# Forward order of a decode step's attention: two V quarters between the products, pair sums and second sums moved ahead, q chunks in halves

## The chip, the cores and the metric

The kernel runs on one core of one Trainium2 chip. The metric is the device time of one execution in microseconds; lower is better. Three executions of the kernel before are known, with a median of 1634.19 us.

## What is computed

The program takes one token through an attention layer and a small MLP mixer, both modulated by a condition vector, and returns the output and the gradients by nine of its inputs. Most of the work is attention over a cache, forward and backward:

```python
Hq, Hkv, Sk, Dh = (32, 32, 8192, 192)         # x is (1, 1, 640)
h = layernorm(x) * (1 + ca) + sa              # ca, sa, ga, ... from silu(c) @ w_mod
q = (h @ wq).reshape(B, Sq, Hq, Dh).transpose(0, 2, 1, 3)
scores = einsum('bhqd,bhkd->bhqk', q, k) * Dh ** (-0.5)
p = softmax(scores)
o = einsum('bhqk,bhkd->bhqd', p, v)
x = x + ga * (o.transpose(0, 2, 1, 3).reshape(B, Sq, Hq * Dh) @ wo)
```

The gradients of K and V are as large as the caches. For the gradient of q the backward part needs, for each head, the matrix sum over positions of p * v (outer) k. The kernel calls it M and makes it in the forward part, so that K is read once; V is read again in the backward part.

## The kernel before

A head's cache of 8192 positions lies as 128 partitions x 64 positions x 192 channels. It is loaded in two halves of 32 positions per partition (1,536 KB each), and V is used in four quarters of 16 positions.

The forward part is one loop of 34 steps (line 393). Step `i` has three heads in hand: `x` is head `i`, whose scores are made; `y` is head `i - 1`, whose softmax and most of whose M are made; `z` is head `i - 2`, whose M is finished. For `x`, each half goes through `dot_mul` (L265, VectorE: K times q over all channels, into the only buffer `prod`), `dot_half` (L270, VectorE: halves the channels), `dot_tree` (L276, TensorE: six matmuls with the identity that add 16 channels at a time in PSUM), and `dot_sum` (L280, VectorE: the last 16 channels). For `y`, `reduce_max` and a matmul `mx` (L418) bring the maximum to all partitions, `negm` (L423) and an exponential on ScalarE (L301) follow; then each V quarter is scaled by the weights in `scale_v`: nine positions on VectorE (L313), seven on ScalarE (L320), into one of three buffers `vs`. `m_quarter` multiplies it on TensorE with K, in three groups of 16 matmuls (L327, L331 for the channels above 128, and L335 for the sums of V itself), and accumulates in PSUM over the four quarters. `m_out` (L338 to L342, ScalarE) and `m_add` (L347, VectorE) take the finished M out.

In odd steps two finished heads form a pair: `pair_sums` (L365 to L367, sixteen small fp32 matmuls), `pair_o` (L372 to L376, VectorE: the reciprocal and o), `pair_ao` (L383, TensorE, copied out by ScalarE at L457) and `e_rows` with `e_rows_out` (L351, L356, and a small write on GpSimd's queue, L357: the weights as rows, for the backward part). All of `po`, `ao_ps`, `er_ps` and `mod_ps` share one PSUM slot. In every fourth step `q_chunk` (L243, L245) makes the q of four heads, two at a time; its PSUM slot is that of `mx`. In steps 1, 5 and 9 `mod_blocks` (L218) makes a part of the modulation instead.

TensorE, VectorE and ScalarE run their instructions in the order in which the code states them: the loop stands in `manual_schedule`. The loads (SyncE's queue, SP in the profile) and GpSimd's queue are ordered by the framework's planner, which goes by its own estimate of when buffers come free. There are five K halves (`KB`), three V halves (`v_sb`), one buffer for a weights chunk (`w_st`) and two for `wo`. So the first K half of head `i + 1` can be loaded when M quarter 3 of head `i - 2` is done, its second one after M quarter 1 of head `i - 1`; V half 0 of head `i` after V quarter 3 of head `i - 2` is scaled, V half 1 of head `i` after V quarter 1 of head `i - 1` is scaled.

In a step, VectorE's order before is: sum of the last half, max, first product, negm, halving, V quarter 0, second product, M add, V quarter 1, second halving, V quarter 2, (pair_o), sum of the first half, V quarter 3. TensorE's is: mx, M quarter 3, first sums, M quarter 0, M quarter 1, (pair sums), second sums, M quarter 2, (AO, rows), (q or modulation).

The backward part (from line 599 on) streams V in and the gradients of V and K out. It isn't touched.

Of the kernel before, what the change touches and what calls it, by code (L numbers as in the profile page):

```python
# [8 lines left out]
FP32 = mybir.dt.float32  # L9
BF16 = mybir.dt.bfloat16  # L10
ALU = mybir.AluOpType
ACT = mybir.ActivationFunctionType
# [8 lines left out]
def kernel(  # L21
# [27 lines left out]
    P = 128  # L49
    D = A_x.shape[-1]  # L50
    _, HQ, S, DH = A_k_cache.shape
# [7 lines left out]
    ND = D // P  # L59
    NF = F // P  # L60
    NQ = QD // P
    NMB = NMOD // P
    NT = HQ // 2
    PW = 2 * DH
    CW = 2 * PW
    VW = DH + 4
    MW = DH + 1
    SCALE = DH ** -0.5
# [3 lines left out]
    V_, A_, T_ = nc.vector, nc.scalar, nc.tensor  # L72
# [7 lines left out]
    psB = ctx.enter_context(tc.tile_pool(name="psB", bufs=1, space=PS))  # L80
# [99 lines left out]
    def load_w(view3, lo, hi):  # L180
        w = wst.tile([P, ND, CW], BF16, name="w_st", tag="w", bufs=1)
        nc.sync.dma_start(out=w[:, :, 0 : hi - lo], in_=view3[:, :, lo:hi])
        return w
# [52 lines left out]

    qs_bc = const.tile([P, QD], BF16, name="qs_bc")

    def q_chunk(n, w):
        for b in range(2):  # L240
            ps = psB.tile([P, 512], FP32, name="q_ps", tag="b")
            for k in range(ND):
                T_.matmul(ps[:, 0:PW], lhsT=ha_bf[:, k : k + 1].to_broadcast([P, P]), rhs=w[:, k, b * PW : (b + 1) * PW], start=(k == 0), stop=(k == ND - 1))  # L243
            lo = n * CW + b * PW
            A_.activation(out=qs_bc[:, lo : lo + PW], in_=ps[:, 0:PW], func=ACT.Copy, scale=SCALE)  # L245

# [9 lines left out]
    def load_v(h, t):  # L258
        v = vp.tile([P, JH, DH], BF16, name="v_sb")
        nc.sync.dma_start(out=v, in_=V_hd[h][:, t * JH : (t + 1) * JH, :])  # L260
        return v
# [24 lines left out]
    with tc.tile_pool(name="kp", bufs=1) as kp, tc.tile_pool(name="vs", bufs=3) as vsp, tc.tile_pool(name="ft", bufs=2) as ft, \  # L286
# [20 lines left out]
        def scale_v(q, v, E4, Ef):  # L307
            vs = vsp.tile([P, JQ, VW], BF16, name="vs")
            j0 = q * JQ
            v0 = (q % 2) * JQ  # L310
            n = JQ - NVA
            A_.copy(out=vs[:, :, DH:VW], in_=E4[:, j0 : j0 + JQ, :])
            V_.tensor_tensor(  # L313
                out=vs[:, 0:n, 0:DH].rearrange("p j (a b) -> p j a b", b=4),
                in0=v[:, v0 : v0 + n, :].rearrange("p j (a b) -> p j a b", b=4),
                in1=E4[:, j0 : j0 + n, None, :].to_broadcast([P, n, DH // 4, 4]),
                op=ALU.mult,
            )
            for k in range(n, JQ):
                A_.activation(out=vs[:, k, 0:DH], in_=v[:, v0 + k, :], func=ACT.Copy, scale=Ef[:, j0 + k : j0 + k + 1])  # L320
            return vs

        def m_quarter(q, kb, vs, mp, op):
            j0 = (q % 2) * JQ
            z = q == 3
            for k in range(JQ):
                T_.matmul(mp[:, 0:MW], lhsT=kb[:, j0 + k, 0:P], rhs=vs[:, k, 0:MW], start=(q == 0 and k == 0), stop=(z and k == JQ - 1), skip_group_check=True)  # L327

            for k in range(JQ):
                p0 = 64 * (k % 2)  # L330
                T_.matmul(mp[p0 : p0 + 64, MO : MO + MW], lhsT=kb[:, j0 + k, P:DH], rhs=vs[:, k, 0:MW], start=False, stop=(z and k >= JQ - 2), skip_group_check=True)  # L331

            for k in range(JQ):
                p0 = 32 * (k % 4)
                T_.matmul(op[p0 : p0 + 32, 0:MW], lhsT=ones_bf, rhs=vs[:, k, 0:MW], start=(q == 0 and k < 4), stop=(z and k >= JQ - 4), skip_group_check=True)  # L335

        def m_out(h, mp, op, os_):
            A_.copy(out=M1[:, h, :], in_=mp[:, 0:MW])  # L338
            mt = ft.tile([P, MW], FP32, name="mt", bufs=1)
            A_.copy(out=mt[64:128, :], in_=mp[64:128, MO : MO + MW])  # L340
            os_[h] = ft.tile([P, MW], FP32, name="osb")
            A_.copy(out=os_[h], in_=op[:, 0:MW])  # L342
            return mt
# [42 lines left out]


        ORDER = {mybir.EngineType.PE, mybir.EngineType.DVE, mybir.EngineType.Activation}
        q_chunk(0, load_w(wq_v, 0, CW))
        mb = MB0  # L390
        X, os_, wo_l = {}, {}, {}
        with tc.manual_schedule(engines=ORDER):
            for i in range(HQ + 2):
                x = X[i] = {} if i < HQ else None
                y = X.get(i - 1) if 0 < i <= HQ else None
                z = X.pop(i - 2) if i > 1 else None
                wch = None
                if x is not None:
                    x["k"] = [load_k(i, 0), load_k(i, 1)]
                    x["v"] = [load_v(i, 0)]  # L400
                    x["S"] = ft.tile([P, J], FP32, name="S_h")
                    qh = qs_bc[:, i * DH : (i + 1) * DH]
                    if i % 2 == 0:
                        wo_l[i // 2] = load_wo(i // 2)
                if i % 4 == 3 and i + 1 < HQ:
                    wch = load_w(wq_v, ((i + 1) // 4) * CW, ((i + 1) // 4 + 1) * CW)
                if i % 4 == 1 and mb < NMB:
                    nb = min(CW // P, NMB - mb)
                    wch = load_w(wm_v, mb * P, (mb + nb) * P)
                if y is not None:  # L410
                    dot_sum(y["d1"], y["S"][:, JH:J])
                    m1 = tcol(1, "m1")
                    V_.reduce_max(out=m1, in_=y["S"], axis=AX.X)
                if x is not None:
                    pa = dot_mul(x["k"][0], qh)
                if y is not None:
                    mx = psB.tile([P, P], FP32, name="mx", tag="b")
                    T_.matmul(mx, lhsT=m1[:, 0:1].to_broadcast([P, P]), rhs=ident_f, start=True, stop=True)  # L418
                if z is not None:
                    m_quarter(3, z["k"][1], z["vs"], z["mp"], z["op"])  # L420
                if y is not None:
                    negm = tcol(1, "negm")
                    V_.reduce_max(out=negm, in_=mx, axis=AX.X, negate=True)  # L423
                    E4, Ef = softmax(i - 1, y["S"], negm)
                if x is not None:
                    dot_half(pa)
                    x["d0"] = dot_tree(pa, psR, DH // 2)
                if y is not None:
                    y["mp"] = psM.tile([P, 512], FP32, name="mp")
                    y["op"] = psO.tile([P, 256], FP32, name="op")  # L430
                    vs = scale_v(0, y["v"][0], E4, Ef)
                if z is not None:
                    mt = m_out(i - 2, z["mp"], z["op"], os_)
                if y is not None:
                    m_quarter(0, y["k"][0], vs, y["mp"], y["op"])
                if x is not None:
                    pb = dot_mul(x["k"][1], qh)
                if z is not None:
                    m_add(i - 2, z["mp"], mt)
                if y is not None:  # L440
                    vs = scale_v(1, y["v"][0], E4, Ef)
                    m_quarter(1, y["k"][0], vs, y["mp"], y["op"])
                if x is not None:
                    x["v"].append(load_v(i, 1))
                last = z is not None and i % 2 == 1
                t = (i - 3) // 2
                if last:
                    po = pair_sums((os_.pop(i - 3), os_.pop(i - 2)))
                if x is not None:
                    dot_half(pb)  # L450
                    x["d1"] = dot_tree(pb, psR, DH // 2)
                if y is not None:
                    vs = scale_v(2, y["v"][1], E4, Ef)
                    m_quarter(2, y["k"][1], vs, y["mp"], y["op"])
                if last:
                    o2 = pair_o(t, po)
                    A_.copy(out=AO[:, :, 2 * t : 2 * t + 2], in_=pair_ao(o2, wo_l.pop(t)))  # L457
                    e_rows_out(t, e_rows(t))
                if wch is not None:
                    if i % 4 == 3:  # L460
                        q_chunk((i + 1) // 4, wch)
                    else:
                        mod_blocks(mb, nb, wch)
                        mb += nb
                if x is not None:
                    dot_sum(x["d0"], x["S"][:, 0:JH])
                if y is not None:
                    y["vs"] = scale_v(3, y["v"][1], E4, Ef)
            while mb < NMB:
                nb = min(CW // P, NMB - mb)  # L470
                mod_blocks(mb, nb, load_w(wm_v, mb * P, (mb + nb) * P))
                mb += nb
# [353 lines left out]
```

## Time and profile before

| | |
|---|---|
| median of three executions | 1634.19 us (1628.32 to 1635.94) |
| the profiled execution | 1626.54 us |
| its span | 1624.7 us |
| busy: PE, DVE, ACT, POOL | 1251.1, 1110.5, 894.3, 108.0 us |
| share of the 16 DMA engines' time: loads, writes | 54.4%, 34.0% |
| read, written | 347.74 MB, 226.43 MB |
| product K times q (L265), 128 x 6144 | 3355 ns each, 64 times |
| V scaling on DVE (L313), one quarter | 1052 ns each, 128 times |

PE is TensorE's matmul side, PEld its weight loads, DVE VectorE, ACT ScalarE, POOL GpSimd, SP SyncE. A line number is that of the kernel before. A wait is idle time of an engine just ahead of an instruction, put down to what released it; idle time of an engine that isn't the bottleneck costs nothing. The clock is the share of full speed that TensorE was granted. Busy time of matmuls is modelled, since they overlap.

### The profile page before, as it was taken

The numbers are of one execution on the slowest core, as the hardware profiler recorded it, in microseconds if no ns is written. First come the engines' busy times: TensorE is split into PE (matmuls) and PEld (weight loads), VectorE is DVE, ScalarE is ACT, GpSimd is POOL, SyncE is SP. The second block draws the span as 40 slices with busy tenths as digits, with TensorE's granted clock in tenths as the row PEclk, the third lists the DMA queues.
The fourth block names the chain that finished last, engine by engine and source line by source line (L and its number), as shares of the span: only waits on it lengthen the run. The fifth ranks groups of instructions, "written<-read, shape, count | busy, mean of one in ns | idle before, by whom it ended". The sixth has DMA issues, their size and how long they took to land.

```text
span 1624.7 us, 28236 instructions
## 1 busy us (share of the span) xinstructions
PE 1251.1 (77%) x11811; PEld 665.3 (41%) x11811; DVE 1110.5 (68%) x1273; ACT 894.3 (55%) x1948; POOL 108.0 (7%) x193
## 2 busy tenths in 40 slices
PE   3888888888888888855784887878677878778774
PEld 1666665666566666642331332322222222222211
DVE  5978777778777878455575757677566665666663
ACT  1656655566666666624563655665455555555544
POOL 0000000000000000011010100111001101010111
PEclk8989999899889999965576656567565555555555
DMA  9888888788778888645899999999999999999988
GB/s 380 348 328 351 356 336 335 311 342 325 314 315 341 329 343 344 238 180 204 346 426 371 374 413 395 399 415 422 392 407 398 396 376 394 360 399 401 402 339 335
DMA packets 76477, 575.99 MB, mean 355 GB/s; under 512 B 7326, under 2 KB 25070, under 8 KB 35390
## 3 DMA queue, kind: packets, MB, share of 16 engines
q1 hardware_dynamic: 51530, 347.23, 54.4%
q0 software_dynamic: 24288, 226.44, 34.0%
q8 instruction: 92, 1.51, 0.4%
q10 hardware_dynamic: 532, 0.53, 0.1%
q14 instruction: 35, 0.29, 0.0%
HBM read 347.74 MB, written 226.43 MB: 353 GB/s over the span
## 4 chain that ended last, share of the span: by engine, by line
issue 35%; PE 28%; DVE 18%; DMA 8%; ACT 6%; POOL 4%; SPq 0%; POOLq 0%; ACTq 0%; DVEq 0%
DVE prod L265 10%; PE dot_ps L276 10%; PE mp L327 6%; PE mp L331 3%; ACT vs L320 3%; DMA w_st<-in_w_mod_dram 2%; DVE vs L313 2%; DMA KB<-in_A_k_cache_dram 2%; PE op L335 2%; DMA out_dram<-dK 2%; DVE prod L270 2%; POOL out_dram L788 1%; POOL out_dram L785 1%; PE po L365 1%; PE dv_ps L726 1%
## 5 line engine op out<-in xcount | busy, mean ns | idle before, releaser
L276 PE MATMUL dot_ps<-prod,ident_bf 128*128 128x512 bf16 x1152 | 470.7, 538 | 65.6 <-DVE prod L265 41.0
L727 ACT CAST dV<-dv_ps 128x768 bf16<-128x768 f32 x512 | 387.8, 809 | 208.0 <-PE dv_ps L726 193.3
L320 ACT ACTIVATE vs<-v_sb,Ef 128x192 bf16<-128x192 bf16 x896 | 323.3, 443 | 0.0
L327 PE MATMUL mp<-vs,KB 128*128 128x193 bf16 x2048 | 229.9, 265 | 80.7 <-DVE vs L313 72.8
L726 PE MATMUL dv_ps<-do_bc,er_b 1*128 1x192 bf16 x2048 | 220.8, 326 | 58.1 <-ACT dV L727 57.3
L265 DVE TENSOR_TENSOR prod<-KB,qs_bc 128x6144 bf16<-128x6144 bf16 x64 | 214.7, 3355 | 65.8 <-PE dot_ps L276 27.1
L327 PEld LDWEIGHTS <-KB 128*128 128x128 bf16 x2048 | 193.8, 105 | 117.5 <-DVE vs L313 80.6
L731 DVE TENSOR_TENSOR dK<-qs_bc,dS 128x6144 bf16<-128x6144 bf16 x64 | 214.2, 3346 | 10.5 <-DMA out_dram<-dK 10.4
L276 PEld LDWEIGHTS <-ident_bf 128*128 128x128 bf16 x1152 | 117.0, 117 | 245.3 <-issue 214.0
L265 DVE TENSOR_TENSOR prod<-v_sb,do_bc 128x6144 bf16<-128x6144 bf16 x64 | 214.3, 3348 | 3.5 <-ACT do_bc L668 3.5
L280 DVE TENSOR_REDUCE dP<-dot_ps 128x32 f32<-128x512 f32 x64 | 44.2, 691 | 237.1 <-PE dot_ps L276 237.1
L726 PEld LDWEIGHTS <-er_b 1*128 1x128 bf16 x2048 | 64.9, 102 | 294.2 <-issue 291.3
L313 DVE TENSOR_TENSOR vs<-v_sb,E 128x1728 bf16<-128x1728 bf16 x128 | 134.5, 1052 | 7.8 <-ACT E L301 7.3
L331 PE MATMUL mp<-vs,KB 128*64 128x193 bf16 x2048 | 116.0, 259 | 0.0
L270 DVE TENSOR_TENSOR prod<-prod 128x3072 bf16<-128x3072 bf16 x64 | 112.0, 1750 | 0.1
L617 PE MATMUL wT_ps<-ident_bf,w_st 128*128 128x128 bf16 (+1 forms) x470 | 51.7, 289 | 69.3 <-DMA w_st<-in_w_mod_dram 25.2
L331 PEld LDWEIGHTS <-KB 128*64 128x64 bf16 x2048 | 87.5, 114 | 27.4 <-issue 27.4
L457 ACT COPY AO<-ao_ps 128x10 f32<-128x10 f32 x16 | 2.7, 169 | 145.5 <-PE ao_ps L383 145.5
L785 POOL DMA_DIRECT2D out_dram<-dV x64 | 35.4, 553 | 660.5 <-ACT dV L727 660.5
L618 ACT COPY wqT<-wT_ps 128x1024 bf16<-128x1024 bf16 (+1 forms) x52 | 50.4, 969 | 49.1 <-PE wT_ps L617 39.6
L617 PEld LDWEIGHTS <-w_st 128*128 128x128 bf16 (+1 forms) x470 | 37.5, 132 | 89.3 <-issue 47.0
L301 ACT ACTIVATE E<-S_h,negm 128x256 bf16<-128x256 f32 x32 | 16.1, 502 | 103.6 <-DVE negm L423 103.6
(207 smaller groups left out, 921.6 us busy)
## 6 DMA issues: line engine op xcount, KB each, us to landing
v_sb<-in_A_v_cache_dram SPq DMA_DIRECT2D x128, 1536.0 KB
KB<-in_A_k_cache_dram SPq DMA_DIRECT2D x64, 1536.0 KB
out_dram<-dV POOLq DMA_DIRECT2D x64, 1536.0 KB, 9.1
out_dram<-dK POOLq DMA_DIRECT2D x64, 1536.0 KB, 13.3
w_st<-in_A_wq_dram SPq DMA_DIRECT2D x16, 960.0 KB
wo_st<-in_A_wo_dram SPq DMA_DIRECT2D x32, 480.0 KB
out_dram<-stg POOLq DMA_DIRECT2D x13, 960.0 KB, 13.9
w_st<-in_w_mod_dram SPq DMA_DIRECT2D x8, 960.0 KB
```

Of the source, the lines that this page charges most:

```text
L265: V_.tensor_tensor(out=prod, in0=src, in1=vec[:, None, :].to_broadcast([P, JH, DH]), op=ALU.mult)
L270: V_.tensor_tensor(out=prod[:, :, 0:w], in0=prod[:, :, 0:w], in1=prod[:, :, w : 2 * w], op=ALU.add)
L276: T_.matmul(ps, lhsT=ident_bf, rhs=prod[:, :, k : k + TS], start=(k == 0), stop=(k == w - TS))
L313: V_.tensor_tensor(out=vs[:, 0:n, 0:DH].rearrange("p j (a b) -> p j a b", b=4), in0=v[:, v0 : v0 + n, :].rearrange("p j (a b) -> p j a b", ...
L320: A_.activation(out=vs[:, k, 0:DH], in_=v[:, v0 + k, :], func=ACT.Copy, scale=Ef[:, j0 + k : j0 + k + 1])
L327: T_.matmul(mp[:, 0:MW], lhsT=kb[:, j0 + k, 0:P], rhs=vs[:, k, 0:MW], start=(q == 0 and k == 0), stop=(z and k == JQ - 1), skip_group_chec ...
L331: T_.matmul(mp[p0 : p0 + 64, MO : MO + MW], lhsT=kb[:, j0 + k, P:DH], rhs=vs[:, k, 0:MW], start=False, stop=(z and k >= JQ - 2), skip_grou ...
L617: T_.transpose(out=tp[lo:hi, (x - x0) * P : (x - x0 + 1) * P], in_=src, identity=ident_bf)
L726: T_.matmul(ps[:, b, k * DH : (k + 1) * DH], lhsT=er[p0 : p0 + 1, 2 * m + k, :], rhs=doh[p0 : p0 + 1, :], start=True, stop=True)
L727: A_.copy(out=dV4[:, 2 * q : 2 * q + 2, m * PW : (m + 1) * PW], in_=ps[:, :, 0:PW])
L731: V_.tensor_tensor(out=out3[:, n0_:n1_, :].rearrange("p j (a b) -> p j a b", b=4), in0=vec.rearrange("p (a b) -> p a b", b=4)[:, None, :, ...
L785: nc.gpsimd.dma_start(out=dV_hd[h][:, js, :], in_=dV)
```

## The change

`q_chunk` becomes `q_half`, which makes the q of two heads. In the loop:

- V quarter 1 is scaled directly after quarter 0, ahead of the second product, and the load of V half 1 is stated right behind it; M quarter 0 stands between the two scalings on TensorE's side.
- The pair sums move ahead of M quarter 1, `pair_o` ahead of the second halving.
- AO, the rows and the q half or modulation move ahead of M quarter 2, which is now the last of the step on TensorE.
- The first q half is made ahead of M quarter 1, the second at the old place.
- A weights chunk is loaded at the end of the even step before, not at the start of the odd step that uses it.

```diff
-    def q_chunk(n, w):
-        for b in range(2):
...
+    def q_half(n, b, w):
...
-                if i % 4 == 3 and i + 1 < HQ:
-                    wch = load_w(wq_v, ((i + 1) // 4) * CW, ((i + 1) // 4 + 1) * CW)
-                if i % 4 == 1 and mb < NMB:
-                    nb = min(CW // P, NMB - mb)
-                    wch = load_w(wm_v, mb * P, (mb + nb) * P)
...
-                    vs = scale_v(0, y["v"][0], E4, Ef)
+                    vs0 = scale_v(0, y["v"][0], E4, Ef)
+                    m_quarter(0, y["k"][0], vs0, y["mp"], y["op"])
+                    vs1 = scale_v(1, y["v"][0], E4, Ef)
+                if x is not None:
+                    x["v"].append(load_v(i, 1))
                 if z is not None:
                     mt = m_out(i - 2, z["mp"], z["op"], os_)
+                if last:
+                    po = pair_sums((os_.pop(i - 3), os_.pop(i - 2)))
+                if i % 4 == 3 and wch is not None:
+                    q_half((i + 1) // 4, 0, wch)
                 if y is not None:
-                    m_quarter(0, y["k"][0], vs, y["mp"], y["op"])
+                    m_quarter(1, y["k"][0], vs1, y["mp"], y["op"])
                 if x is not None:
                     pb = dot_mul(x["k"][1], qh)
                 if z is not None:
                     m_add(i - 2, z["mp"], mt)
-                if y is not None:
-                    vs = scale_v(1, y["v"][0], E4, Ef)
-                    m_quarter(1, y["k"][0], vs, y["mp"], y["op"])
-                if x is not None:
-                    x["v"].append(load_v(i, 1))
...
                 if last:
-                    po = pair_sums((os_.pop(i - 3), os_.pop(i - 2)))
+                    o2 = pair_o(t, po)
                 if x is not None:
                     dot_half(pb)
                     x["d1"] = dot_tree(pb, psR, DH // 2)
                 if y is not None:
                     vs = scale_v(2, y["v"][1], E4, Ef)
-                    m_quarter(2, y["k"][1], vs, y["mp"], y["op"])
                 if last:
-                    o2 = pair_o(t, po)
                     A_.copy(out=AO[:, :, 2 * t : 2 * t + 2], in_=pair_ao(o2, wo_l.pop(t)))
                     e_rows_out(t, e_rows(t))
-                if wch is not None:
-                    if i % 4 == 3:
-                        q_chunk((i + 1) // 4, wch)
-                    else:
-                        mod_blocks(mb, nb, wch)
-                        mb += nb
+                if i % 4 == 3 and wch is not None:
+                    q_half((i + 1) // 4, 1, wch)
+                    wch = None
+                if i % 4 == 1 and wch is not None:
+                    mod_blocks(mb, nb, wch)
+                    mb += nb
+                    wch = None
+                if i % 4 == 2 and i + 2 < HQ:
+                    wch = load_w(wq_v, ((i + 2) // 4) * CW, ((i + 2) // 4 + 1) * CW)
+                if i % 4 == 0 and mb < NMB:
+                    nb = min(CW // P, NMB - mb)
+                    wch = load_w(wm_v, mb * P, (mb + nb) * P)
+                if y is not None:
+                    m_quarter(2, y["k"][1], vs, y["mp"], y["op"])
```

More of the change, by code (lines that the diff above doesn't have):

```diff
@@ L237 @@
     qs_bc = const.tile([P, QD], BF16, name="qs_bc")
-    def q_chunk(n, w):
-        for b in range(2):
[L241 to L245, printed above, removed]
+    def q_half(n, b, w):
+        ps = psB.tile([P, 512], FP32, name="q_ps", tag="b")
+        for k in range(ND):
+            T_.matmul(ps[:, 0:PW], lhsT=ha_bf[:, k : k + 1].to_broadcast([P, P]), rhs=w[:, k, b * PW : (b + 1) * PW], start=(k == 0), stop=(k == ND - 1))
+        lo = n * CW + b * PW
+        A_.activation(out=qs_bc[:, lo : lo + PW], in_=ps[:, 0:PW], func=ACT.Copy, scale=SCALE)
     E_all = const.tile([P, HQ, J], BF16, name="E_all")
@@ L388 @@
         ORDER = {mybir.EngineType.PE, mybir.EngineType.DVE, mybir.EngineType.Activation}
-        q_chunk(0, load_w(wq_v, 0, CW))
+        w = load_w(wq_v, 0, CW)
+        for b in range(2):
+            q_half(0, b, w)
         mb = MB0
         X, os_, wo_l = {}, {}, {}
+        wch = None
         with tc.manual_schedule(engines=ORDER):
@@ L396 @@
                 z = X.pop(i - 2) if i > 1 else None
-                wch = None
+                last = z is not None and i % 2 == 1
+                t = (i - 3) // 2
                 if x is not None:
@@ L439 @@
                     m_add(i - 2, z["mp"], mt)
-                if y is not None:
-                    vs = scale_v(1, y["v"][0], E4, Ef)
-                    m_quarter(1, y["k"][0], vs, y["mp"], y["op"])
-                if x is not None:
-                    x["v"].append(load_v(i, 1))
-                last = z is not None and i % 2 == 1
-                t = (i - 3) // 2
                 if last:
-                    po = pair_sums((os_.pop(i - 3), os_.pop(i - 2)))
+                    o2 = pair_o(t, po)
                 if x is not None:
@@ L453 @@
                     vs = scale_v(2, y["v"][1], E4, Ef)
-                    m_quarter(2, y["k"][1], vs, y["mp"], y["op"])
                 if last:
-                    o2 = pair_o(t, po)
                     A_.copy(out=AO[:, :, 2 * t : 2 * t + 2], in_=pair_ao(o2, wo_l.pop(t)))
                     e_rows_out(t, e_rows(t))
-                if wch is not None:
-                    if i % 4 == 3:
-                        q_chunk((i + 1) // 4, wch)
-                    else:
-                        mod_blocks(mb, nb, wch)
-                        mb += nb
+                if i % 4 == 3 and wch is not None:
[4 more added lines that the diff above has]
+                    mb += nb
+                    wch = None
+                if i % 4 == 2 and i + 2 < HQ:
[5 more added lines that the diff above has]
+                    m_quarter(2, y["k"][1], vs, y["mp"], y["op"])
                 if x is not None:
```

## The prediction

> **What bounds the kernel now.** I read the page's slices first, then busy time by stretch, then the waits inside the forward part, then the order of time of four of its steps.
>
> ```profile
> span 1624.7 us, 28236 instructions
> ...
> PEclk8989999899889999965576656567565555555555
> DMA  9888888788778888645899999999999999999988
> ...
> 0.00:684.00 684.00, 555.82 (x7280) 408.75 (x7281) 524.02 (x499) 396.62 (x1260) 9.36 (x23) 0.92 0.84 332
> 684.00:760.00 76.00, 41.86 (x517) 30.58 (x515) 34.22 (x125) 25.65 (x49) 8.33 (x13) 0.62 0.52 190
> 760.00:1625.00 865.00, 653.42 (x4017) 225.92 (x4016) 552.24 (x650) 472.03 (x642) 90.34 (x157) 0.58 0.96 387
> ```
>
> The columns of the last three are PE, PEld, DVE, ACT, POOL, then clock, DMA share, GB/s. The change touches only the first stretch, where no engine is full: PE 81%, DVE 77%, DMA 84%. Past 760 us the DMA engines are at 0.96 and nothing changes. So the question is what DVE, the engine with the longest chain per head, waits for in the forward part. The waits of 60 to 640 us, 28 heads, in us, times, longest:
>
> ```profile
> DVE rz L372 <- PE po L367: 38.4, 14, 4.1
> DVE prod L265 <- PE dot_ps L276: 22.4, 26, 1.5
> DVE prod L265 <- ACT qs_bc L245: 20.6, 5, 5.1
> DVE S_h L280 <- PE dot_ps L276: 16.6, 12, 1.6
> DVE prod L265 <- DMA KB<-in_A_k_cache_dram: 12.3, 6, 3.3
> ...
> PE mp L327 <- DVE vs L313: 66.2, 28, 2.9
> ```
>
> How long a step is, I take from `negm`, once per step (here steps 20 to 24), on the timeline:
>
> ```profile
> 430.78 0.28 DVE L423 TENSOR_REDUCE negm<-mx 128x1 f32<-128x128 f32 x1
> 449.24 0.28 DVE L423 TENSOR_REDUCE negm<-mx 128x1 f32<-128x128 f32 x1
> 470.70 0.29 DVE L423 TENSOR_REDUCE negm<-mx 128x1 f32<-128x128 f32 x1 [0.33 <-PE mx L418]
> 491.02 0.28 DVE L423 TENSOR_REDUCE negm<-mx 128x1 f32<-128x128 f32 x1
> 513.87 0.28 DVE L423 TENSOR_REDUCE negm<-mx 128x1 f32<-128x128 f32 x1
> ```
>
> Steps of 18.46, 21.46, 20.32 and 22.85 us. From start to start on the same timeline DVE's own work is: negm 0.2, halving 1.67, four V scalings 0.98 each, products 3.39 and 3.27, M add 0.35, second halving 1.67, two sums 0.65 and 0.72, max 0.14: **16.0 us**, and 0.65 more for the pair in odd steps. The rest is waits: step 20 is 16.0 + 0.85 (product on the sums) + 1.55 (sum on the sums) = 18.4; step 21 is 16.65 + 0.58 + 3.74 (the pair) + 0.33 = 21.3. The account closes. Negm runs from 35.9 to 672.4 us, 31 steps of 20.5: **82.1 us for four**.
>
> **What the Trainium skill says.** "TensorE: Matmul & The Clock Gate", Part 1: after an idle window of about 3.4 us PE runs at half rate. The trace agrees, with a shorter idle: after the 2.33 us that M quarter 1 waits for its V, its first 16 matmuls take 2.77 us and not 1.52. The same page, on the engine queues (the architectural detail): ACT and DVE are strict first-in-first-out. "DMA: Bandwidth & Descriptors", the anatomy of a DMA: waits on semaphores happen in the issuing queue before dispatch. Its section on queues and rings: an engine takes a ring's descriptors in order, so a K half issued behind a V half lands behind it. The trace shows this: with several queued, landings follow 3.7 to 3.8 us apart; one alone lands 6.2 us after issue (V 164.88 to 171.03).
>
> **The change part by part.** I write the new orders down from negm = 0, with the durations above.
>
> *Two V quarters between the products.* Only the place of quarter 1 changes, no instruction is added. The second product waited 22.4/28 = 0.8 us a step for the first sums to leave `prod`; the 0.98 us of quarter 1 now covers that. M quarter 1 stood behind the second product through its V, 66.2/28 = 2.36 us of PE idle a step, and half rate after it. Now ACT goes E4 and its two copies 0.27 to 1.1, quarter 0 to 3.7, quarter 1 to 6.3, M copies to 7.2; PE does first sums to 3.2, M quarter 0 to 5.9, and in an even step quarter 1 to 8.9, at 2.7 each (494.31 to 497.06 on the timeline). The halving of the second product ends at 9.3, so the sums follow at once, to 10.6, before DVE wants them at 11.9: the 16.6 us of sum waits goes in even steps. **Even step: 16.0.** PE holds 4 x 2.7 + 2 x 1.3 + 0.4 = 13.8. If that cover is gone (half rate), each block of 16 costs 1.25 more.
>
> *The pair sums earlier.* They need the M copies: 7.2, then 2.0 on PE (502.06 to 504.09) to 9.2. DVE is free after the M add at 7.6 and `pair_o` (L372) waits 1.6, against 38.4/14 = 2.7 before. But now the second halving stands behind this wait: 9.85 to 11.5. M quarter 1 stands behind the pair sums on PE (and behind a q half, 1.0), and the next K half, which needs its buffer, behind that.
>
> *Second sums, then AO, rows, q or mod ahead of M quarter 2.* Odd step without q: M quarter 1 to 11.9, sums to 13.2, AO 0.47, the rows and two ACT copies to 14.2, quarter 2 to 16.9, mx 17.3; DVE ends its product at 18.3, so **18.4**. Odd step with q: 1.0 later, another 1.0 for the second half, mx 19.3 and DVE waits for it: **19.4**. The ACT copy of AO stands behind V quarter 2 on ACT, done by 10; free. The mod chunk (30 matmuls, three times in all) is about 1 us under the product.
>
> *q in two halves.* 20.6 us in 5 waits of 4.1 disappear: the first two heads' q is there half a step before. What takes its place is the mx wait, 1.0, counted above. ACT's work is the same, 0.49 each.
>
> *The weights load a step earlier.* It leaves the start of an odd step, and on SP passes from behind V half 0 to behind V half 1 of the even step. It takes the same 3.5 us of the ring. V half 1's issue comes 3.4 us earlier, since its buffer is free with quarter 1. POOL's row write has nothing beside it.
>
> *Bounds on DMA.* Four steps move 16 x 1,536 + 2 x 480 + 2 x 960 KB = 28.1 MB; the stretch from 150 to 190 us, at share 0.90, moved 357 GB/s, so 397 when full: **70.8 us for four**, 68 with one weights load. The trace of before doesn't show such density; with K waits of nothing the sum below is 72.3, with those of before doubled 75.9. I take before's, 12.3/7 = 1.8 per four.
>
> **Sum.** 16.0 + 18.4 + 16.0 + 19.4 = 69.8; half rate in the two odd steps, where the pair sums (one column each) keep PE little busy, one block each, 2 x 1.25 = 2.5; K waits 1.8: **74.1 us for four**. 31 steps: 574, against 636.5: -62 us. The profiled execution took 1626.54 (span 1624.7) and would take 1564; the median of the three runs is 1634.19, 7.6 above it, so **1572**.
>
> **Rivals.** The loads are not in the hand-written order: a planner places them on SP by its own guess of when buffers come free.
>
> ```profile
> 443.64 0.33 SPq L260 DMA_DIRECT2D v_sb<-in_A_v_cache_dram  x1
> 450.25 0.33 SPq L296 DMA_DIRECT2D KB<-in_A_k_cache_dram  x1
> 457.65 0.33 SPq L260 DMA_DIRECT2D v_sb<-in_A_v_cache_dram  x1
> 461.39 0.33 SPq L296 DMA_DIRECT2D KB<-in_A_k_cache_dram  x1
> ```
>
> This is V, then the next head's first K half ahead of V half 1, though the program has it after. That is worth much, and in steps with a weights load (485.90) it is V, V, K, K.
>
> A, the sum above: K keeps its place. For it: K's buffer frees with M quarter 3 (K is issued 1.0 and 1.9 after negm, at 450.25 and 432.70), V's with quarter 1 on ACT (6.3). Against: the margin shrinks from 6.7 us (432.70 to 439.43) to 4.4. 0.68.
>
> B: K loses it in one step of four, the one with the weights load. V half 1 issues at 6.3, lands at 12.4, K behind it at 16.2, where the product wanted it at 12.7: 3.5, and 1 of knock-on: 31/4 x 4.5 = 35 back, 1607. 0.15.
>
> C, slower: K loses it in every step. Each then lasts at least 16.2 + 3.3 = 19.5, four 78, the weights load in front of K 3.5, half rate and K waits 4: 85.5, so 663, +26: 1660. It decides where the planner thinks that two V quarters end before M quarter 3. For it: quarter 1 no longer hangs behind that quarter on PE. Against: 4.4 us of margin. This is also how the change could fail to do what it says: the orders on PE, DVE and ACT are fixed in the code, that of the loads isn't. 0.11.
>
> D: PE becomes the bound at half rate in every odd step, and the waits come back as mx waits of 5 us: 74.1 + 2 x 3.5 = 81.1, -8: 1626, about no change. Against: PE has no long idle left. 0.06.
>
> **Numbers.** Fast end: the DMA floor, 31/4 x 70.8 = 549, -88: 1547; A's own range is 1552 to 1596. With B the 80% range is 1553 to 1626; C and the edges are left out. Half a per cent, 8 us, is about what can be told from no change. Faster 0.82 (A, nearly all of B), same 0.07, slower 0.11.
>
> **What would show it.** Steps of 16 and 18 to 20 us by negm; no wait of the product on q or on the sums; M quarter 1 no longer idle for V; pair wait 1.6; DMA share near 0.95 in a forward part that ends near 622 us; K ahead of V half 1 on SP. Wrong if the product waits for K in most steps (B, C), or if negm waits for mx over 2 us (D).

## The result and the profile after

| | before | after |
|---|---|---|
| median of four executions each | 1631.26 us | 1648.33 us (1645.26 to 1649.97) |
| ratio, with its 95% interval | | 1.0104 [1.0064, 1.0145] |
| span of the profiled execution | 1624.7 us | 1646.9 us |

The change made the kernel 1% slower, by 17 us, where 62 us less were forecast. In the code of after the helpers stand one line higher: the product is L264, the wait for the pair L371, the load of a V half L259, that of a K half L295.

First the busy time by stretch (columns as before: PE, PEld, DVE, ACT, POOL, clock, DMA share, GB/s), of the kernel after:

```profile
0.00:708.00 708.00, 547.12 (x7300) 410.05 (x7301) 521.64 (x499) 399.22 (x1264) 9.35 (x23) 0.87 0.84 321
785.00:1647.00 862.00, 651.74 (x4005) 225.30 (x4003) 549.43 (x647) 469.48 (x639) 90.07 (x156) 0.58 0.96 388
```

The loss is all in the forward part: it ends 24 us later (708 us, not 684), and the backward part still takes 862 to 865. The forward part holds the same work (DVE 521.64 us busy, 524.02 before) at a lower clock and a lower DMA rate, 321 GB/s where 332 was. So the time is waiting, and the waits of 60 to 640 us say for what (in us, times, longest; 27 heads):

```profile
PE dot_ps L275 <- DVE prod L269: 122.0, 32, 9.5
DVE prod L264 <- DMA KB<-in_A_k_cache_dram: 91.3, 14, 8.0
...
DVE rz L371 <- PE po L366: 25.2, 13, 2.5
...
DVE prod L264 <- PE dot_ps L275: 11.3, 13, 0.9
...
DVE S_h L279 <- PE dot_ps L275: 7.8, 6, 1.6
```

Every wait that was forecast to go or shrink did: the product's wait for q (20.6 us) is no longer in the list, its wait for the sums fell from 22.4 to 11.3, the sum's own from 16.6 to 7.8, the pair's from 38.4 to 25.2. Together that is 54 us less. The product's wait for K took more than that back: 12.3 us became 91.3, in 14 waits of 6.5 on average, one for every second head. TensorE, in turn, waits for the halved product, L269 (122.0 us).

Steps by `negm`, on the timeline of the kernel after (start, duration; steps 19 to 22 lie between the five):

```profile
424.27 0.28 DVE L421 TENSOR_REDUCE negm<-mx 128x1 f32<-128x128 f32 x1
446.16 0.29 DVE L421 TENSOR_REDUCE negm<-mx 128x1 f32<-128x128 f32 x1 [0.43 <-PE mx L416]
466.90 0.28 DVE L421 TENSOR_REDUCE negm<-mx 128x1 f32<-128x128 f32 x1
485.81 0.28 DVE L421 TENSOR_REDUCE negm<-mx 128x1 f32<-128x128 f32 x1
509.58 0.28 DVE L421 TENSOR_REDUCE negm<-mx 128x1 f32<-128x128 f32 x1
```

The steps last 21.9 (odd, with q), 20.7 (even), 18.9 (odd) and 23.8 us (even): 85.3 for four. From the first `negm` (37.25) to the last (697.40) it is 660.1 us for 31 steps, 85.2 for four, against 82.1 before. The even steps, which had the least to do, are now among the longest. What they wait for stands in SyncE's queue, first in the even step from 446.16, then in the one from 485.81 (start, duration, what is issued, how many):

```profile
452.59 0.33 SPq L259 DMA_DIRECT2D v_sb<-in_A_v_cache_dram  x1
453.01 2.28 SPq L295 DMA_DIRECT2D KB<-in_A_k_cache_dram  x2
...
492.23 0.33 SPq L259 DMA_DIRECT2D v_sb<-in_A_v_cache_dram  x1
492.60 0.43 SPq L182 DMA_DIRECT2D w_st<-in_A_wq_dram  x1
493.08 1.37 SPq L295 DMA_DIRECT2D KB<-in_A_k_cache_dram  x2
```

and in the first product of these two steps on VectorE (the bracket is the idle time before it and its releaser):

```profile
463.62 3.36 DVE L264 TENSOR_TENSOR prod<-KB,qs_bc 128x6144 bf16<-128x6144 bf16 x1 [4.56 <-DMA KB<-in_A_k_cache_dram]
...
506.31 3.36 DVE L264 TENSOR_TENSOR prod<-KB,qs_bc 128x6144 bf16<-128x6144 bf16 x1 [7.79 <-DMA KB<-in_A_k_cache_dram]
```

In the first of the two, V half 1 is issued ahead of the next head's two K halves. It has to wait until quarter 1 is scaled, 6.4 us after `negm` (452.59 - 446.16), and K's first half stands behind it in the queue, although its own buffer is long free. K then lands behind V in the rings (V at 459.9, K at 463.6 by the semaphores in the trace), and the product starts 17.5 us after `negm` (463.62 - 446.16). In the even step after that, from 485.81, the weights chunk stands between V and K, and the product starts 20.5 us after `negm`. In odd steps K's first half keeps its place. So of two steps one is lost: every even step from 2 to 30, fifteen in all, nine of them with a weights chunk in front of K too.

### The profile page after: what moved, and what is told of

Its sections match the earlier page's. It is cut to its first block, busy times and chain, and to the rows that moved or that the text cites. A ratio compares the mean times of both kernels' runs of the same rounds, so it can differ in the third digit from the quotient of the medians.

```text
span 1646.9 us, 28215 instructions
## 1 busy us (share of the span) xinstructions
PE 1240.7 (75%) x11811; PEld 665.2 (40%) x11811; DVE 1107.8 (67%) x1273; ACT 895.8 (54%) x1948; POOL 108.3 (7%) x193
## 3 DMA queue, kind: packets, MB, share of 16 engines
q8 instruction: 92, 1.51, 0.4%
## 4 chain that ended last, share of the span: by engine, by line
issue 35%; PE 23%; DMA 18%; DVE 12%; ACT 7%; POOL 4%; SPq 1%; POOLq 0%; ACTq 0%; DVEq 0%
DMA KB<-in_A_k_cache_dram 12%; PE dot_ps L275 7%; DVE prod L264 6%; PE mp L326 5%; ACT vs L319 4%; DVE prod L269 2%; DMA w_st<-in_w_mod_dram 2%; PE mp L330 2%; DMA out_dram<-dK 2%; DMA w_st<-in_A_wq_dram 1%; POOL out_dram L793 1%; POOL out_dram L790 1%; PE po L364 1%; ACT dV L732 1%; PE dv_ps L731 1%
## 5 line engine op out<-in xcount | busy, mean ns | idle before, releaser
L275 PE MATMUL dot_ps<-prod,ident_bf 128*128 128x512 bf16 x1152 | 480.3, 548 | 186.5 <-DVE prod L269 145.5
L264 DVE TENSOR_TENSOR prod<-KB,qs_bc 128x6144 bf16<-128x6144 bf16 x64 | 214.7, 3355 | 120.2 <-DMA KB<-in_A_k_cache_dram 102.7
L275 PEld LDWEIGHTS <-ident_bf 128*128 128x128 bf16 x1152 | 118.7, 117 | 374.3 <-issue 347.9
L326 PE MATMUL mp<-vs,KB 128*128 128x193 bf16 x2048 | 219.0, 265 | 0.5 <-ACT vs L319 0.5
L264 DVE TENSOR_TENSOR prod<-v_sb,do_bc 128x6144 bf16<-128x6144 bf16 x64 | 214.3, 3348 | 3.5 <-ACT do_bc L673 3.5
L269 DVE TENSOR_TENSOR prod<-prod 128x3072 bf16<-128x3072 bf16 x64 | 112.1, 1751 | 0.6
L330 PE MATMUL mp<-vs,KB 128*64 128x193 bf16 x2048 | 112.1, 253 | 0.0
L334 PE MATMUL op<-vs,ones_bf 128*32 128x193 bf16 x2048 | 66.2, 250 | 0.0
```

The source lines that it names most:

```text
L264: V_.tensor_tensor(out=prod, in0=src, in1=vec[:, None, :].to_broadcast([P, JH, DH]), op=ALU.mult)
L269: V_.tensor_tensor(out=prod[:, :, 0:w], in0=prod[:, :, 0:w], in1=prod[:, :, w : 2 * w], op=ALU.add)
L275: T_.matmul(ps, lhsT=ident_bf, rhs=prod[:, :, k : k + TS], start=(k == 0), stop=(k == w - TS))
```

## The experiments

Two theories were put against each other. **Theory 1:** the order of the loads alone is the cause; the new order on the engines does what the prediction worked out. **Theory 2:** the new engine order loses by itself (half rate, longer chains, PSUM slots), and K's wait only stands where another would. Where a run's expectation speaks of "the sum", it is the prediction's 74.1 us for four steps.

### K's first half stated early, in the kernel after

```diff
-                    x["k"] = [load_k(i, 0), load_k(i, 1)]
+                    x["k"] = [load_k(0, 0) if i == 0 else k0, load_k(i, 1)]
...
                     m_quarter(3, z["k"][1], z["vs"], z["mp"], z["op"])
+                if i + 1 < HQ:
+                    k0 = load_k(i + 1, 0)
```

Only one load is moved, right behind the quarter that frees its buffer. Nothing on PE, DVE or ACT changes.

> The changed kernel, with one statement moved: the load of the next head's first K half is stated behind M quarter 3, so that it stands ahead of V half 1 on SP in every step (in the changed kernel it stands behind it in every even step). Orders on PE, DVE and ACT are those of the changed kernel. Theory 1 (the place of that load is the whole cause of the loss; the new compute order is worth what the prediction's sum says): steps of 16 us after even and 18 to 20 after odd, four in about 74, no wait of the product on K above 2 us, about 1572 us, ratio to before 0.96. Theory 2 (the new compute order itself costs, for instance through M quarter 2 behind AO and q on PE): the waits for K go, but time stays at 1625 us or more.

Measured: **1520.75 us**, 0.9334 [0.9292, 0.9376] of before: 127.6 us below the change as it was made, from the place of one load (125.6 from the first to the last `negm`). Theory 2 falls. The forward part of this kernel by busy time:

```profile
0.00:582.00 582.00, 513.93 (x7328) 392.42 (x7328) 519.00 (x499) 400.58 (x1268) 9.33 (x23) 0.98 0.97 392
```

and its waits from 60 to 560 us, about 29 heads:

```profile
DVE prod L264 <- DMA KB<-in_A_k_cache_dram: 22.8, 14, 2.9
...
DVE rz L371 <- PE po L366: 3.5, 5, 0.9
DVE S_h L279 <- PE dot_ps L275: 2.1, 3, 0.9
```

The same work as after (DVE 519.00 us) is done in 582 us and not 708, with the DMA engines at 0.97 and the clock at 0.98. The three waits together are 28 us, where the kernel after has 136 in the four shown. SyncE's queue in the even step that begins at 330.95:

```profile
332.04 0.33 SPq L295 DMA_DIRECT2D KB<-in_A_k_cache_dram  x1
337.37 0.33 SPq L259 DMA_DIRECT2D v_sb<-in_A_v_cache_dram  x1
337.74 0.44 SPq L182 DMA_DIRECT2D w_st<-in_A_wq_dram  x1
339.26 0.33 SPq L295 DMA_DIRECT2D KB<-in_A_k_cache_dram  x1
```

K is issued 1.1 us after `negm`, then V half 1 at 6.4, the weights, and K's second half. This even step lasts 15.9 us (to 346.85).

### The same edit in the kernel before

> The kernel before with the same statement moved: K's first half ahead of V half 1 also in the steps that load a weights chunk, where the kernel before has it behind. Theory 1: before's waits for K (12.3 us in 28 heads) mostly go and nothing else: about 1620 to 1630 us, ratio 0.99 to 1.0. If the order of loads is worth much also without the new compute order, 1600 or less.

Measured: 1628.78 us, 0.9979 [0.9952, 1.0006]: no difference. K's wait did go (2.7 us from 60 to 600, 12.3 in the kernel before), but the wait for q grew from 20.6 to 26.1, and those for the pair and the sums stayed (35.6, 23.1, 16.4). With the loads where the kernel before has them, K was not what bound. The 2.5 us gained here can't be set against the 127.6: before, K is behind V half 1 in nine odd steps only, those with a weights load, and after in fifteen even ones. The next run puts it behind in the same steps.

### The loads' order of after, in the kernel before

The engine order is the old one, as is the place of the weights load. SyncE is put under the hand-written order too; K's first half is stated behind M quarter 3 in odd steps (the first added line) and behind the load of V half 1 in even ones (the second).

```diff
-        ORDER = {mybir.EngineType.PE, mybir.EngineType.DVE, mybir.EngineType.Activation}
+        ORDER = {mybir.EngineType.PE, mybir.EngineType.DVE, mybir.EngineType.Activation, mybir.EngineType.SP}
...
+                if i % 2 == 1 and i + 1 < HQ:
+                    k0 = load_k(i + 1, 0)
...
+                if i % 2 == 0 and i + 1 < HQ:
+                    k0 = load_k(i + 1, 0)
```

> The kernel before with SP held to the changed kernel's order of K and V loads: in even steps V half 1 first, then K. Compute order as before. Theory 1: V half 1 is issued some 8.7 us after negm (its buffer frees behind the second product), lands 6.1 later and K 3.8 behind that, at 18.6, and the product ends 3.3 after: even steps of about 22 instead of 19.5, 16 of them, +40: about 1670 us, ratio 1.025. Theory 2: about 1634, the order of loads alone costs little.

Measured: 1698.56 us, 1.0419 [1.0376, 1.0462]. The product's two longest waits from 60 to 640 us:

```profile
DVE prod L265 <- DMA KB<-in_A_k_cache_dram: 58.2, 13, 6.1
DVE prod L265 <- PE dot_ps L276: 39.9, 26, 1.8
```

Even steps last 21.9 to 24.9 us (16.7 to 20.3 before). It loses more than expected: beside K's wait, which grew by 46 us, the product's wait for the sums grew from 22.4 to 39.9. This order of the loads thus makes either engine order slow. With the old engine order it costs 70 us against K early (1698.56 and 1628.78), with the new one 127.6. And the new engine order, with its own place of the weights load, is 50 us faster than the old under it (1698.56 to 1648.33), and 108 with K early (1628.78 to 1520.75). So each order is worth something by itself, and more with the other.

### The weights load back at its old place, in the kernel after

The loads are left to the planner, as in after; only the statement of the weights load goes back to the start of the odd step.

```diff
+                if i % 4 == 3 and i + 1 < HQ:
+                    wch = load_w(wq_v, ((i + 1) // 4) * CW, ((i + 1) // 4 + 1) * CW)
...
-                if i % 4 == 2 and i + 2 < HQ:
-                    wch = load_w(wq_v, ((i + 2) // 4) * CW, ((i + 2) // 4 + 1) * CW)
```

(The two lines for the modulation chunk go with it in the same way.)

> The changed kernel with one part undone: the weights chunk is stated at the start of the odd step again, as before. K's load is where the changed kernel states it; the planner now places it ahead of V half 1 in the even steps, and behind it in the odd steps with a weights load. Theory 1 (the moved weights load is what cost K its place in the even steps, and that was the loss): even steps back to 16 to 17, four in about 74 to 77: 1565 to 1590 us. Rival (early release of V's buffer alone does it): 1630 or more.

Measured: 1561.32 us, 0.9572 [0.9535, 0.9608]. SyncE's queue from an even step (first three lines) into the odd one after it, on this kernel's timeline:

```profile
165.88 0.33 SPq L259 DMA_DIRECT2D v_sb<-in_A_v_cache_dram  x1
...
167.94 0.33 SPq L295 DMA_DIRECT2D KB<-in_A_k_cache_dram  x1
172.98 0.33 SPq L259 DMA_DIRECT2D v_sb<-in_A_v_cache_dram  x1
...
179.37 0.43 SPq L182 DMA_DIRECT2D w_st<-in_w_mod_dram  x1
189.45 0.33 SPq L259 DMA_DIRECT2D v_sb<-in_A_v_cache_dram  x1
189.83 4.16 SPq L295 DMA_DIRECT2D KB<-in_A_k_cache_dram  x2
```

K's first half is ahead of V half 1 in the even step (167.94, 172.98) and behind it in the odd step with the weights chunk. K's wait is 20.0 us in 13 waits (60 to 560 us). So it was the move of the weights load that cost K its place in the even steps. By which reckoning the planner turned the two loads around is not shown: in after they are turned around also in the six even steps that hold no weights chunk. With the weights load where it was, 87 of the 127.6 us are back. Of the other 40, 17 are what the old place costs by itself (next run); the rest lies with K's place in the odd steps, and from step 13 on with V halves that the planner puts elsewhere. It was not taken apart further.

### The weights load back, with K stated early

> e1 (K first in every step) with the weights chunk stated at the start of the odd step again. The chunk is then issued behind V half 0 of the odd step, some 3 us ahead of negm, and lands 9 to 10 after, about when the first q half is due at 9.2. Theory 1 (the earlier weights load is worth little by itself): within 10 us of e1, 1515 to 1531. If the q half waits on it: 2 to 3 us in 7 steps, 1535 to 1540.

Measured: 1537.83 us, 0.9416 [0.9367, 0.9465]: 17 us above the kernel with K early. The first q half now waits for its weights, and the sums stand behind it. From 60 to 560 us:

```profile
DVE S_h L279 <- PE dot_ps L275: 22.3, 9, 3.9
...
PE q_ps L242 <- DMA w_st<-in_A_wq_dram: 7.7, 7, 1.7
```

The earlier weights load is thus right for q. It is dear only through what the planner made of it. The loads of this run stand in the same order, weights included, as those of the kernel before with K early (1628.78): the 91 us between these two are the worth of the engine order alone.

### K second to V half 1 in one step of four

Rival B by itself: in the kernel with K early, in steps with `i % 4 == 2` alone (eight steps), K's first half is stated behind V half 1's load; the weights chunk comes after it.

```diff
-                if i + 1 < HQ:
+                if i % 4 != 2 and i + 1 < HQ:
                     k0 = load_k(i + 1, 0)
...
                     x["v"].append(load_v(i, 1))
+                if i % 4 == 2 and i + 1 < HQ:
+                    k0 = load_k(i + 1, 0)
```

> e1 with K's first half behind V half 1 in one step of four alone, the even step that loads a q chunk (8 steps); the weights chunk is behind K there. The dose between e1 (no step) and the changed kernel (16 steps, 127 us). Rival B of the prediction priced one such step at 4.5 us: +36, 1557 us. The traces of the changed kernel say 4.8 in the step itself (20.7 without a weights load in front of K, against 15.9) and about 2 in the one after: +54, 1575 us.

Measured: 1569.55 us, 0.9601 [0.9575, 0.9628]: 49 us for eight steps, **6.1 us a step**. From the first to the last `negm` alone it is 5.4 (577.8 against 534.5 us); what lies outside that stretch differs by some us between executions. In after it is 127.6 / 15 = **8.5** (8.4 by `negm`), where nine of the fifteen have the weights chunk in front of K too.

### K's second half ahead of the weights chunk

In the kernel with K early:

```diff
-                    x["k"] = [load_k(0, 0) if i == 0 else k0, load_k(i, 1)]
+                    x["k"] = [load_k(0, 0) if i == 0 else k0, load_k(0, 1) if i == 0 else k1]
...
+                if i + 1 < HQ:
+                    k1 = load_k(i + 1, 1)
                 if i % 4 == 2 and i + 2 < HQ:
```

> e1 with K's second half stated ahead of the weights chunk too. The waits of the product on K left in e1 (22.8 us in 14, in the steps after a weights load) should go. But DMA was busy 0.97 of the forward part in e1: if bytes set the pace, 1512 to 1525; if order still does, 22 us less: about 1500.

Measured: 1519.75 us, 0.9296 [0.9281, 0.9311], the same as with K early alone. The waits changed places, without effect: K's fell to 4.9 us, the pair's rose to 13.7: DMA share 0.97 and 392 GB/s up to 582 us, to the digit those of the kernel with K early. Both stand at what the loads need: the 31 steps hold 31 x 4 halves of 1,536 KB, 15.5 loads of `wo` of 480 KB and ten weights chunks of 960 KB, 212.5 MB; at the 397 GB/s of 100 to 560 us this is 535 us, and from the first to the last `negm` the kernel with K early takes 534.5. The rate is of the same trace, so this sum only accounts for the bytes; that the loads bind is read from the DMA share of 0.98. The prediction had worked out the same 397 from the kernel before (357 GB/s at share 0.90).

### Each part of the change undone, with K early

Four kernels, each with one part of the engine order back where it was: V quarter 1, its matmuls and the load of V half 1 behind the second product; the pair sums behind M quarter 1 and `pair_o` behind V quarter 2; M quarter 2 ahead of AO, rows and q; both q halves at the old place. A fifth is the kernel before with K early and quarter 1 scaled ahead of the second product, nothing else. The first as a diff:

```diff
                     m_quarter(0, y["k"][0], vs0, y["mp"], y["op"])
-                    vs1 = scale_v(1, y["v"][0], E4, Ef)
-                if x is not None:
-                    x["v"].append(load_v(i, 1))
...
-                if y is not None:
-                    m_quarter(1, y["k"][0], vs1, y["mp"], y["op"])
...
                     m_add(i - 2, z["mp"], mt)
+                if y is not None:
+                    vs1 = scale_v(1, y["v"][0], E4, Ef)
+                    m_quarter(1, y["k"][0], vs1, y["mp"], y["op"])
+                if x is not None:
+                    x["v"].append(load_v(i, 1))
```

Quarter 1 undone:

> e1 (changed kernel, K first) with V quarter 1 and M quarter 1 back behind the second product; everything else as in e1. Theory 1 (the two V quarters are the main gain): the product waits 0.6 to 0.9 for the sums again, M quarter 1 waits about 2.3 for its V and the second sums come late: even steps 18.4 instead of 16.0, odd ones 1 longer, four in 75.5: +50, about 1570 us. Rival (the gain of e1 is that of the loads' and the pair's order): within 10 us of e1, 1520 to 1531.

The pair undone:

> e1 with the pair sums back behind M quarter 1 and the pair's VectorE part back behind V quarter 2. The prediction's sum gave this move 1.1 us a pair. By the new order alone it should be worth less: M quarter 1 ends at 8.9, pair sums 2.0, so 10.9, and VectorE asks at 10.3: a wait of 0.6 where e1 has 5.2 us in 7. Theory 1: within 8 us of e1. If the move mattered, 16 pairs by 1 to 2 us: 1537 to 1553.

M quarter 2 undone:

> e1 with M quarter 2 back ahead of AO, rows, q and modulation on TensorE. TensorE's sum in a step is the same, mx comes no later; but ScalarE's copies of AO and rows wait 2.7 us longer and V quarter 3 stands behind them. Theory 1: odd steps 1 to 2 us longer, 16 of them, 1537 to 1553. If nothing waits for V quarter 3: same as e1.

The q halves undone:

> e1 with both q halves at the old place, behind AO and rows. Theory 1: the first product of the next step waits for the first q half again, some 2 us net in 7 steps, about +14: 1535. If DMA is what now sets the pace of four steps, less: within 8 us.

Quarter 1 alone, on before:

> The kernel before with two edits alone: V quarter 1 directly behind quarter 0 (M quarter 1 ahead of the second product's M add on TensorE), and K first in every step as in e2. Pair sums, AO, M quarter 2, q chunk and weights load as before. Theory 1, from the parts undone: e1 + 41 (M quarter 2) + 16 (q halves) + 3 (pair) = about 1580 us; even steps 17 to 18, odd ones with q 22. If the parts help one another, more: 1595 or above.

| | us | ratio to before | above K early (1520.75) | DMA, 100 to 560 us |
|---|---|---|---|---|
| quarter 1 undone | 1568.69 | 0.9608 [0.9566, 0.9651] | 48 | 366 GB/s |
| pair undone | 1523.49 | 0.9338 [0.9293, 0.9383] | 3, not told from none | 397 |
| M quarter 2 undone | 1561.66 | 0.9567 [0.9524, 0.961] | 41 | 373 |
| q halves undone | 1536.97 | 0.942 [0.9379, 0.9462] | 16 | 392 |
| quarter 1 alone, on before | 1567.47 | 0.9606 [0.9558, 0.9655] | 47 | 371 |

In the first four the loads stand in the same order as with K early, and in the fifth as in the kernel before with K early, so these differences are due to the engine order. Quarter 1 undone brings its waits back: the sum's 23.9 us, the product's for the sums 15.2 (60 to 560 us). The q halves undone bring steps with q of 20.2 us. The pair's earlier place is worth nothing here: the loads already run at 397 GB/s with either. M quarter 2 is worth more than the 16 to 32 us expected, and in its even steps too (17.2 to 18.1 us), where nothing stands between the old and the new place. The waits of DVE and of SyncE's queue in this kernel (60 to 560 us) say where it goes:

```profile
DVE prod L264 <- DMA KB<-in_A_k_cache_dram: 34.7, 27, 3.5
...
SPq L259 <- ACT vs L319: 177.5, 54, 8.2
```

With K early alone the queue's wait for ACT's V scaling, in front of a V load, is 132.6 us in 58, and the product's for K 22.8 in 14. V half 0 of an even step, whose buffer V quarter 3 on ACT frees, is issued 1.5 to 2.4 us after `negm` where with K early it is at most 0.1 after, and K's first half behind it at 2.6 to 3.5 where it is 1.1 to 2.1. A V load that waits for its buffer thus holds the K load behind it. That the late quarter on ACT starts this chain is argued from these times; no run isolates it, and K's wait holds only 12 of the 41 us.

Quarter 1 alone, with K early, takes 61 us from the kernel that has only K early (1628.78); the other parts give the remaining 47.

## Why the prediction was wrong

**The step that failed** is the choice of rival A, "K keeps its place", at 0.68. It was argued from margins of time in the trace (K's buffer free at 1.0 us, V's at 6.3, "the margin shrinks from 6.7 us to 4.4"). K's buffer was indeed free at 1.1 us and V's at 6.4, as the run with K early and the kernel after show; but the planner's order didn't follow these times. The same section had the better evidence: "in steps with a weights load (485.90) it is V, V, K, K". Before, that pattern went with the place of the weights load, and the change moves the weights load.

**The term that was priced wrong** is that load: "It takes the same 3.5 us of the ring", at no cost. As bytes this held (3.0 us more until the product starts, 20.5 against 17.5). But its move had the planner put V half 1 ahead of K in the even steps, where the product has the least else to wait for; the run with the weights load back shows it, with K first again in those steps and 87 of the 127.6 us regained. B named this loss, but for one step in four; it came in one of two.

**Sizes.** B's 4.5 us for a lost step ("3.5, and 1 of knock-on") measured 5.4 to 6.1 alone and 8.5 in after. The 3.5 was low since V landed not at 12.4 but at 13.7, and K not at 16.2 but at 17.4. In the steps of after, 4.6 of the even step with no weights (20.7 against 16.1), 7.9 of the one with (23.8 against 15.9) and 1.5 and 2.3 of the odd step that follows are lost; six steps of the first kind and nine of the second make 128. C's price for the place, 16.2 + 3.3, was within 1.3 us of the even step (20.7). V half 1's issue moved by 2.0 to 4.0 us (from 8.4 to 10.4 after `negm` to 6.4), for which the prediction has 3.4 in one place and 2.3 in another (6.7 to 4.4).

**Luck.** C's number came nearest, 85.5 for four where 85.2 were measured. That is luck: it had K lose its place in every step, at 19.5 each, where K lost it in the even steps alone, which last 19.7 to 24.1 us, and the odd ones 18.8 to 22.1.

**Without the loss, the sum was right part by part and too slow in all.** With K early four steps take 17.36, 15.90, 19.59 and 16.09 us, 68.9 in all:

| term | predicted | measured, K early |
|---|---|---|
| even step | 16.0 | 15.90, 16.09 |
| odd step without q | 18.4 | 17.36 |
| odd step with q | 19.4 | 19.59, of which K 1.59, sums 0.87, mx 0.43 |
| wait for the pair | 1.6 | 0.94 |
| half rate in odd steps | 2.5 for four | 0.87 in these four, as the wait for the sums; clock 0.98 |
| K waits | 1.8 for four | inside the steps above |
| 31 steps | 574 | 534.5 |

The sum's four steps without the two terms added on top, 69.8, were within 1 us of the 68.9 measured; the half rate (2.5) and K's waits (1.8) made it 74.1. The half rate on the path is small: the three waits for the sums, 2.1 us in 29 heads, each stand behind a block of M quarter 1 that took 2.03 to 2.62 us and not 1.51. Nor did a pause of 2.33 us bring it each time in the trace of before, as the prediction read from one such pause:

```profile
457.61 2.77 PE L327 MATMUL mp<-vs,KB 128*128 128x193 bf16 x16 [2.33 <-DVE vs L313]
...
499.38 1.52 PE L327 MATMUL mp<-vs,KB 128*128 128x193 bf16 x16 [2.33 <-DVE vs L313]
```

Of the 26 pauses of 2.32 or 2.33 us there, 13 were followed by the full rate. The pair's first ten matmuls (ten for each head in the trace, twenty in all, not sixteen) use only the earlier head's sums and start before the last M copy (319.57 and 320.55 with K early), so `pair_o` waits less, 0.94 us at most in these four steps. B's 1607 and the measured 1648 are nearer each other than their terms are: the sum was 40 us too slow (574 for 534.5) and the loss 93 too small (35 for 127.6). The offset of 7.6 us from the profiled execution to the median is not there with K early (1520.99 and 1520.75).

**The floor** was 70.8 us for four, and the kernel with K early is below it: it counted two weights chunks in each four, where past step 9 there is one (its 68 for that case stands against 68.9). The sentence that the trace of before shows no such density was right about the trace, not about the chip.

**Worth of the parts.** Undoing the V quarters and the q halves cost what their runs were expected to, from the prediction's durations. The pair was priced as a gain of about 1 us a pair and gave none, with the loads at 397 GB/s in both kernels. M quarter 2 had no price of its own, and is worth 41 us. All this was measured with K early; what the parts are worth one by one under after's order of loads was not run.

The rule of the Trainium skill that the prediction drew on, "DMA: Bandwidth & Descriptors", the anatomy of a DMA, is that a wait on a semaphore is served in the issuing queue, before dispatch. The trace agrees: in after K is issued 6.9 us after `negm` (453.01 - 446.16), with K early 1.1 us after, and the 5.8 between are spent in SyncE's queue behind a V load that waits for its buffer.

## What to carry to other kernels

Before an engine order is priced, write down the order of the loads on their queue, and state it by hand where it matters: with the load that the path needs next ahead of one that has to wait for a buffer. A load that is moved is to be followed past every other load of its queue, since where a planner orders them the move can turn around two others; look for the pattern in the steps of the old trace that already have that load in that place. And an order of work and an order of loads are worth more together than alone: against the kernel before, K early alone showed no gain (0.998), the engine order with what the planner made of the loads a small loss (1.010), and both together a gain of nearly 7% (0.933). So a part that shows no gain is not yet shown to be useless.

## What was not expected of the hardware

- One core moved 397 GB/s, DMA share 0.98, over 460 us, mostly in loads of 1,536 KB, while the engines were busy at 0.92 (PE) and 0.93 (DVE). Before the change the same stretch had 333. The first line is of the kernel with K early, the second of the kernel before (columns as above):

```profile
100.00:560.00 460.00, 420.92 (x6064) 324.42 (x6065) 429.11 (x397) 331.86 (x1053) 7.01 (x13) 0.98 0.98 397
100.00:560.00 460.00, 386.80 (x5124) 287.36 (x5124) 363.22 (x334) 278.59 (x888) 5.94 (x11) 0.93 0.84 333
```

- TensorE's half rate stands behind the long waits: in after, all 17 full blocks of six sum matmuls (L275) behind a wait of 5.0 to 9.5 us take 2.72 us, and all those behind a wait of 0.65 us or less take 1.45 or 1.46. The mean clock of the forward part fell to 0.87 from 0.92; with the waits gone it is 0.98. That the slow blocks lengthen later waits is not shown by itself.
